# The first quarter of two weight matrices in four equal pieces, its fold by halves, v's sums by pairs of heads, and the opening in a new order

## The chip, the cores and the metric

The kernel runs on one core of a Trainium2 chip. A core has five engines with a queue each: TensorE (PE) for matrix products, VectorE (DVE), ScalarE (ACT) and GpSimd (POOL) for elementwise work and reductions, and SyncE (SP), which here issues the loads and stores. The metric is the device time of one execution in microseconds. The kernel before took 639.45 us, the median of three runs (638.46 to 640.53).

## What is computed

An attention with 32 memory slots per head, over 8 batches, 8 heads, 576 positions and 64 channels, and then a two-layer network on all 4608 tokens. The weights of the network are float64 in memory; q, k, v and phi are float32.

```python
a = exp(phi - max(phi, axis=2)); a = a / (sum(a, axis=2) + 1e-09)
k_m = einsum('bhsm,bhsd->bhmd', a, k)
v_m = einsum('bhsm,bhsd->bhmd', a, v)
scores = matmul(q, k_m.T) / sqrt(64)
attn = exp(scores - max(scores)); attn = attn / (sum(attn) + 1e-09)
x = matmul(attn, v_m)            # as [4608, 512]
h = x @ w_in                     # 512 x 2048
out = maximum(0.01 * h, h) @ w_out
```

## The kernel before, in words

The attention's last product and the first layer are folded into one: per batch b and quarter j of the 2048 inner columns, `fold_products` multiplies v_m (in `vT`) by that quarter of w_in. The up products (`up_products`, L1160 in the opening) then multiply these folded weights by the attention weights `a`, `leaky` (L1169) applies the nonlinearity, and the down products (`down_products`, L1244) multiply by a quarter of w_out and add up in PSUM. Batch 0's first tokens are worked in full float32 in the opening, with the weights as they come in; later groups use pairs of float16 halves.

The weights need work before use. A quarter of w_in or w_out (`weights("i", j)`, `weights("o", j)`) is 128 rows of 2048 float64. It is loaded in pieces of 768, 768 and 512 elements to each of the 128 partitions (`ld`), the low word is converted (`h`, on ScalarE at L392 where `OPENING_ACT` lists the piece, on VectorE at L394 where not), the high word is converted on ScalarE (`y`, L403), and VectorE puts both together into the float32 tile (`t`, the put, L412). `b` sums squares of a finished quarter on ScalarE. The pieces are staged in eight slots of `arena` that are used in turn (`ld_slot`), by q and by the next batch's phi, k and v as well: a load can be issued only when the work that read the slot's last content is done.

Nothing is scheduled by a tool. Every step has a name, and two strings, `OPENING` and `LATER`, list the steps in the order in which they are issued; each engine does its own instructions in that order. `a0.` and `a1.` are steps of the attention of batches 0 and 1: phi, k, v and q loads, `A` the maximum of phi, `B` its exponential, `C` the sums over positions (`C10` for k, `C11` for v, both by `slots_of`, L706), `D` transposes and the copy `vT` (`D5`), `E` the scores (`E10` and `E1`, L879) and their transposes into `t` (`E2`, L890), `S` the softmax in chunks, which ends for the first chunk in the transpose into `a` (`S06`, L969). `f00.1` is the fold of quarter 0 (L1036) and `f00.2` its two copies on ScalarE into `w_mem` (L1453). `u0.P0` is an up product, `u0.V0` its nonlinearity, `u0.O0` its down product. `z.1` and `z.4` are dummy products on PE (L1467), 128 or 512 columns wide, whose result nobody reads. `LATER` lists the rest of the program.

Of the kernel before, what the change touches and what calls it, by code (L numbers as in the profile page):

```python
# [44 lines left out]
o0.t0 f00.2 u0.P1 i1.ld0 i1.h0 o1.ld2 u0.P0 i1.h1 i1.y0 u0.V1 a0.D2 o0.ld1 o0.ld2 i1.y1 u1.P0 i1.h2
o2.ld2 u1.P1 i1.t0 u0.V0 o1.ld1 i1.t2 i1.t1 u0.O0 f01.1 i2.ld2 o0.h1 o1.h2 o0.y1 i2.ld1 u1.V0 o0.y2
o2.h2 o1.y2 o0.t1 a0.S11 o0.h2 i2.y2 f01.2 u1.O0 a0.S12 a0.S13 u0.O1 i2.y1 u1.V1 o1.t2 o0.t2 o1.ld0
i2.ld0 i2.h1 o1.y1 i2.h2 o2.y2 a0.S14 i2.t2 o2.ld0 o2.t2 a0.S15 u2.P0 u2.P1 a0.S16 i2.h0 i3.ld1
o1.h0 i2.t1 a1.phi o1.h1 o1.t1 u2.V0 u1.O1 i2.y0 o1.y0 i2.t0 o2.h0 A0.h i1.b a1.kv1 a1.kv0 o1.t0
u3.P0 u2.V1 i3.y1 u2.O0 o2.y0 i2.b u3.V0 a1.kv2 i3.h1 a0.D4 a1.A1 a1.kv3 a1.A2 a1.A3 u3.P1 a1.B0  # L50
i3.t1 a1.B10 a1.q1 a1.B20 f02.1 o2.t0 u3.O0 f02.2 a1.B3 a1.C10 a1.C2 a1.C30 u5.P0 o0.b a1.C31
o2.ld1 a1.q0 u3.V1 u4.P1 o1.b u5.V0 a1.C4 a1.D11 u4.P0 a1.C3k o2.h1 i3.ld0 a1.D2 A0.l a1.Q1 a1.Q0
a1.D10 a0.S17 o2.y1 i3.ld2 o3.ld0 a1.D3 u4.V0 i3.y0 a1.D5 u2.O1 i3.y2 i3.h0 a1.D4 o2.t1 i3.h2 u4.V1
i3.t0 a2.phi i3.t2 a1.E1 u3.O1 i3.b a1.E21 o3.h0 u4.O0 a1.E20 o3.ld1 ci.1 o2.b a1.S11 a2.A1 ci.2
W03.p o3.y1 a1.S01 o3.h1 o3.t1 o3.ld2 a0.S18 u5.P1 o3.y2 a2.kv2 o3.h2 ci.3 u5.O0 ci.4 o3.t2 u4.O1
o3.y0 e0. o3.t0 W03.h1 u5.V1 W03.l1 a2.A2 a1.S02 W03.h0 e1. a1.S03 W03.l0 o3.s0 o3.b u6.P0 co.1
# [1502 lines left out]
```

## Time and profile before

| What | us |
|---|---|
| median of 3 runs | 639.45 (638.46 to 640.53) |
| the profiled execution, whole | 639.44 |
| its span in the profile | 637.3 |
| PE busy | 628.7 |
| VectorE busy | 526.8 |
| ScalarE busy | 399.2 |
| first up products start | 27.91 |

All other times are read from the profile of one execution, counted from the start of its span. PE is busy for 99% of the span; its busy time includes the dummy products of the opening. The granted clock of PE reads 1.00 of full speed in every stretch.

### The profile page before, as it was taken

The numbers are of one execution on the slowest core, as the hardware profiler recorded it, in microseconds if no ns is written. First come the engines' busy times: TensorE is split into PE (matmuls) and PEld (weight loads), VectorE is DVE, ScalarE is ACT, GpSimd is POOL, SyncE is SP. The second block draws the span as 40 slices with busy tenths as digits, with TensorE's granted clock in tenths as the row PEclk, the third lists the DMA queues.
The fourth block names the chain that finished last, engine by engine and source line by source line (L and its number), as shares of the span: only waits on it lengthen the run. The fifth ranks groups of instructions, "written<-read, shape, count | busy, mean of one in ns | idle before, by whom it ended". The sixth has DMA issues, their size and how long they took to land.

```text
span 637.3 us, 17457 instructions
## 1 busy us (share of the span) xinstructions
PE 628.7 (99%) x7408; PEld 489.2 (77%) x7408; DVE 526.8 (83%) x887; ACT 399.2 (63%) x690; POOL 32.4 (5%) x38
## 2 busy tenths in 40 slices
PE   8999999999999999999999999999999999999997
PEld 4545446665568888888888888889888888998886
DVE  5868899999998999996988887889877886766473
ACT  3799889777757546565566636646655646455471
POOL 0011110110010001000010001100200010000000
PEclk9999999999999999999999999999999999999999
DMA  8999612262343433503332224012242100010101
GB/s 311 405 372 319 245 46 51 75 114 89 103 102 71 150 60 72 170 12 73 71 108 64 55 46 103 19 51 76 84 77 34 36 1 19 17 35 1 35 23 45
DMA packets 85182, 61.18 MB, mean 96 GB/s; under 512 B 62064, under 2 KB 67440, under 8 KB 85104
## 3 DMA queue, kind: packets, MB, share of 16 engines
q1 hardware_dynamic: 84720, 59.80, 33.0%
q8 instruction: 58, 0.95, 0.6%
q10 hardware_dynamic: 384, 0.26, 0.2%
q14 instruction: 20, 0.16, 0.1%
HBM read 50.59 MB, written 9.45 MB: 94 GB/s over the span
## 4 chain that ended last, share of the span: by engine, by line
PE 90%; DMA 3%; DVE 3%; ACT 2%; issue 1%; SPq 1%; DVEq 0%; ACTq 0%
PE po L1354 34%; PE ph L1293 23%; PE po L1244 12%; PE ph L1160 6%; PE ph L1354 6%; PE pa L1036 4%; PE pa L706 3%; DMA arena<-in_moe_w_in_dram 2%; PE pa L863 1%; DMA arena<-in_phi_dram 1%; ACT arena L403 1%; PE ph L879 1%; DVE arena L1323 0%; ACT arena L392 0%; DVE r1k L600 0%
## 5 line engine op out<-in xcount | busy, mean ns | idle before, releaser
L1354 PEld LDWEIGHTS <-arena 128*128 128x128 f16 x2352 | 227.1, 98 | 30.4 <-issue 4.2
L1306 ACT ACTIVATE wi<-ph,g_sc 128x256 f32<-128x256 f32 x224 | 97.6, 472 | 151.8 <-PE ph L1293 148.4
L1293 PE MATMUL ph<-a,w_mem 128*128 128x256 f16 (+3 forms) x1512 | 147.3, 245 | 0.0
L1354 PE MATMUL po<-wo,arena 128*128 128x256 f16 x1008 | 130.3, 273 | 0.1
L1354 PE MATMUL po<-arena 128*128 128x256 f16 x1008 | 130.1, 273 | 0.0
L1293 PEld LDWEIGHTS <-w_mem 128*128 128x128 f16 x1512 | 119.0, 98 | 13.6 <-issue 4.2
L1244 PE MATMUL po<-wo,arena 128*128 128x512 f16 (+1 forms) x348 | 96.4, 425 | 0.0
L1331 DVE TENSOR_TENSOR arena<-arena 128x1024 f16<-128x1024 f32 x56 | 69.5, 1241 | 30.4 <-ACT arena L1327 30.4
L1327 ACT CAST arena<-arena 128x1024 f16<-128x1024 f32 x56 | 58.6, 1046 | 11.6 <-DVE arena L1323 11.1
L1331 DVE TENSOR_TENSOR arena<-wi,arena 128x768 f16<-128x768 f32 x56 | 54.2, 970 | 14.0 <-ACT arena L1327 13.2
L1244 PEld LDWEIGHTS <-arena 128*128 128x128 f16 x276 | 26.2, 98 | 30.4 <-issue 2.5
L1323 DVE TENSOR_TENSOR arena<-wi,arena 128x256 f32<-128x256 f32 x112 | 47.4, 423 | 1.9
L1327 ACT CAST arena<-wi 128x768 f16<-128x768 f32 x56 | 46.5, 833 | 3.8 <-PE po L1354 2.8
L1323 DVE TENSOR_TENSOR arena<-wi 128x256 f32<-128x256 f32 x112 | 45.7, 449 | 3.4 <-ACT wi L1306 2.1
L1354 PE MATMUL ph<-wo,arena 128*128 128x256 f16 x336 | 45.4, 273 | 0.0
L1160 PE MATMUL ph<-a,w_mem 128*128 128x192 f16 (+2 forms) x288 | 42.0, 293 | 0.8 <-ACT w_mem L1453 0.8
L1001 POOL TENSOR_TENSOR a<-t,a 128x1024 f16<-128x1024 f32 (+2 forms) x16 | 22.2, 1404 | 397.7 <-ACT a L996 344.0
L1075 DVE SCALAR_TENSOR_TENSOR w_mem<-pa,w_mem 128x512 f16<-128x512 f32 x40 | 26.3, 680 | 4.0 <-ACT w_mem L1069 4.0
L1160 PEld LDWEIGHTS <-w_mem 128*128 128x128 f16 x264 | 23.4, 98 | 7.3 <-issue 1.6
L1036 PE MATMUL pa<-wi,vT 64*32 64x512 f16 (+1 forms) x704 | 28.9, 420 | 0.0
L1169 ACT ACTIVATE arena<-ph,g_sc 128x384 f32<-128x384 f32 (+1 forms) x32 | 16.7, 525 | 15.6 <-PE ph L1160 12.5
L1069 ACT ACTIVATE w_mem<-pa 128x512 f16<-128x512 f32 x40 | 23.3, 596 | 5.0 <-PE pa L1036 4.1
(229 smaller groups left out, 752.0 us busy)
## 6 DMA issues: line engine op xcount, KB each, us to landing
out_dram<-obs SPq DMA_DIRECT2D x136, 64.0 KB, 1.7
arena<-in_k_dram SPq DMA_DIRECT2D x28, 288.0 KB, 3.7
arena<-in_v_dram SPq DMA_DIRECT2D x28, 288.0 KB, 3.9
arena<-in_q_dram SPq DMA_DIRECT2D x96, 72.0 KB, 2.9
arena<-in_moe_w_in_dram SPq DMA_DIRECT2D x12, 512.0 KB, 8.1
arena<-in_moe_w_out_dram SPq DMA_DIRECT2D x8, 768.0 KB, 8.0
arena<-in_phi_dram SPq DMA_DIRECT2D x7, 576.0 KB, 4.6
arena<-in_q_dram SPq DMA_DIRECT2D x4, 576.0 KB, 6.8
```

What stands on the lines that cost most here:

```text
L1001: nc.gpsimd.tensor_tensor(piece(lo, tb), piece(t2, tb), piece(hi, tb), ALU.subtract)
L1036: nc.tensor.matmul(pf[g][cols, :], lhs, rhs, start=(n == 0), stop=(n == len(passes) - 1), tile_position=(g * D, hh * M),)
L1069: nc.scalar.activation(tiles(halves(w16(b, j), g)[:, 0]), w(g), AF.Copy, scale=ws)
L1075: nc.vector.scalar_tensor_tensor(tiles(t[:, 1]), w(g), ws, tiles(t[:, 0]), ALU.mult, ALU.subtract)
L1160: nc.tensor.matmul(ph[:, t0:t0 + n * sb], lhs, rhs, start=(m == 0), stop=(m == len(seq) - 1))
L1244: nc.tensor.matmul(pos["32" if full(G, u) else G][t], lhs, rhs, start=(f == 2 * u0 and m == 0), stop=(f == 2 * u1 - 1 and m == len(seq) - 1),)
L1293: nc.tensor.matmul(ph[:, t0:t0 + n], lhs, rhs, start=(m == 0), stop=(m == len(seq) - 1))
L1306: nc.scalar.activation(dst, ph, AF.Prelu, scale=g_sc2[:, j:j + 1], alpha=SLOPE)
L1323: nc.vector.tensor_tensor(gt[:, x], y, z, op)
L1327: nc.scalar.copy(dst[:, 0], src)
L1331: nc.vector.tensor_tensor(dst[:, 1], src, dst[:, 0], ALU.subtract)
L1354: nc.tensor.matmul(acc, g[:, x, s, u], rhs, start=(h == 0 and k % NQ == 0 and u == 0 and m == 0), stop=(k % NQ == NQ - 1 and u == 1 and m ...
```

## The change

Quarter 0 of each weight matrix is loaded in four pieces of 512 elements per partition. For w_in a piece is two of the four row blocks by half of the quarter's columns, so the first two pieces hold the first half of the columns; for w_out a piece is one block of 128 rows, and the rows of that quarter are dealt to the partitions in another way (`w_out_0`, `by_tile`). The fourth piece of each has a place of its own outside the eight slots. The fold of quarter 0 is made in two halves of columns with two half copies each (`f00.10`, `f00.11`), and v's sums for two heads at a time (`C110`, `C111`), with v's loads in two steps (`v0`, `v1`). `OPENING` is listed anew, `OPENING_ACT` moves conversions of low words between ScalarE and VectorE; `LATER` is the same. (`half` and the steps `u0.P00` and the like are defined and not listed.)

```diff
-a0.phi0 z.4 a0.phi1 z.4 a0.A10 z.4 a0.A11 a0.k a0.A2 a0.A3 z.1 z.1 a0.B0 a0.B10 a0.B20 a0.B11
+a0.phi0 a0.A10 z.4 a0.phi1 a0.A11 z.4 a0.k z.4 a0.A2 a0.A3 a0.q1 a0.B0 z.4 a0.B10 z.1 i0.ld0 a0.B20
...
 OPENING_ACT = {
-    "i0": (0, 1, 2), "i1": (2,), "i2": (2,), "i3": (2,), "o0": (0, 1, 2), "o1": (0, 1, 2),
-    "o2": (0, 1, 2), "o3": (0, 1, 2),
+    "i0": (0, 1, 2),
+    "i1": (0,),
+    "i2": (),
+    "i3": (2,),
+    "o0": (0,),
+    "o1": (1,),
+    "o2": (0, 2),
+    "o3": (0, 1),
 }
...
+    w_out_0 = w_out.rearrange("(j f p) e -> j p f e", p=P, j=NQ)[0]
+    HQ = FQ // 2
...
         def load(i):
+            if j == 0:
+                n = E
+                st = ld_slot() if i < 3 else at(G_OLD + 4 * 3072 if kind == "i" else W_OLD, 8 * n)
+                st = st.bitcast(I64)
+                if kind == "o":
+                    nc.sync.dma_start(st[:, 0:n], w_out_0[:, i])
+                else:
+                    cs, fs = slice(i % 2 * 2, i % 2 * 2 + 2), slice(i // 2 * HQ, (i // 2 + 1) * HQ)
+                    nc.sync.dma_start(
+                        st[:, 0:n].rearrange("p (c f) -> p c f", c=2), src[:, cs, fs]
+                    )
+                return views(i, st, n)
...
+                steps[f"{name}v{i}"] = lambda i=i: [load_kv(hh, (1,)) for hh in (2 * i, 2 * i + 1)]
...
+            steps[f"{name}C10"] = lambda: slots_of((0,))
             for i in range(2):
-                steps[f"{name}C1{i}"] = lambda i=i: slots_of((i,))
+                steps[f"{name}C11{i}"] = lambda i=i: slots_of((1,), range(2 * i, 2 * i + 2))
...
-    def fold_products(b, j):
+    def fold_products(b, j, f0=0, f1=FQ):
...
-        pf = [ps_a.tile([P, FQ], F32, name="pa") for g in range(NG)]
+        pf = [ps_a.tile([P, f1 - f0], F32, name="pa") for g in range(NG)]
...
-                    fs = slice(hh * FQ, (hh + 1) * FQ)
+                    fs = slice(hh * FQ + f0, hh * FQ + f1)
...
+    def half_products(h):
+        first["f", 0, h] = fold_products(0, 0, h * HQ, (h + 1) * HQ)
+
+    for h in range(2):
+        steps[f"f00.1{h}"] = lambda h=h: half_products(h)
+        for g in range(NG):
+            steps[f"f00.2{h}{g}"] = lambda h=h, g=g: nc.scalar.copy(
+                w32[0][g][:, h * HQ:(h + 1) * HQ], first["f", 0, h][g]
+            )
```

What the new order makes of it is seen at three places. Line numbers of the changed kernel are higher by about 40. The first is PE's queue at the start of the up products (L1160 before, L1203 after); L790 and L830 are x_v's transpose, L1467 and L1526 dummies, L1036 and L1076 the fold, L1244 and L1287 down products. Before:

```order
L790 MATMUL pa<-ident,x_v 128x128
L1467 MATMUL po<-ones 128x512
L1036 MATMUL pa<-wi_89,vT 32x512 x8
L1160 MATMUL ph<-a,w_mem 128x384 x4
L350 MATMUL pa<-mdiag,ones 128x128
L1160 MATMUL ph<-a,w_mem 128x384 x4
L1244 MATMUL po<-wo_91,arena 128x512 x3
L1036 MATMUL pa<-wi_88,vT 32x512 x8
```

And after:

```order
L830 MATMUL pa<-ident,x_v 128x128
L1526 MATMUL po<-ones 128x512
L1076 MATMUL pa<-wi_89,vT 32x256 x8
L1526 MATMUL po<-ones 128x128 x2
L1203 MATMUL ph<-a,w_mem 128x384 x4
L1076 MATMUL pa<-wi_89,vT 32x256 x8
L1287 MATMUL po<-wo_91,arena 128x512 x3
L1203 MATMUL ph<-a,w_mem 128x384 x4
```

Half of the fold now stands behind the first two up products.

The second place is SP's queue from the second half of q on; `wo_92` to `wi_86` are the places of k and v for the four pairs of heads. Before:

```order
L589 DMA arena<-in_q_dram 128x2x576
L382 DMA arena<-in_moe_w_in_dram 128x512
L382 DMA arena<-in_moe_w_in_dram 128x256
L382 DMA arena<-in_moe_w_in_dram 128x512
L555 DMA wo_92<-in_v_dram 128x576
L555 DMA wo_93<-in_v_dram 128x576
L555 DMA wo_94<-in_v_dram 128x576
L555 DMA wi_86<-in_v_dram 128x576
L378 DMA arena<-in_moe_w_out_dram 128x768
```

And after:

```order
L628 DMA arena<-in_q_dram 128x2x576
L402 DMA arena<-in_moe_w_in_dram 128x2x256
L593 DMA wo_92<-in_v_dram 128x576
L593 DMA wo_93<-in_v_dram 128x576
L593 DMA wo_94<-in_v_dram 128x576
L593 DMA wi_86<-in_v_dram 128x576
L402 DMA arena<-in_moe_w_in_dram 128x2x256
L399 DMA arena<-in_moe_w_out_dram 128x512
L402 DMA arena<-in_moe_w_in_dram 128x2x256
L399 DMA arena<-in_moe_w_out_dram 128x512
```

One piece stands ahead of q's second half in both (not shown); v now comes ahead of the other two pieces of the quarter.

The third place is VectorE's queue from the scores' transposes on (L890 before, L930 after); L412 and L449 are puts, L961 and L1001 the scaling, L969 and L1009 the transpose into `a`. Before:

```order
L890 STREAM_TRANSPOSE t_299<-pa 128x96 x3
L944 TENSOR_REDUCE tm<-t_299 128x24
L947 TENSOR_TENSOR t_299<-t_299,tm 128x768
L412 SCALAR_TENSOR_TENSOR wi_89<-arena 128x768
L956 TENSOR_REDUCE ts__399<-t_299 128x24
L957 TENSOR_SCALAR ts__399<-ts__399 128x24
L958 RECIPROCAL ts__399<-ts__399 128x24
L761 TENSOR_SCALAR x_v<-po,r_228 128x64 x2
L961 TENSOR_TENSOR t_299<-t_299,ts__399 128x768
L769 TENSOR_REDUCE l_409<-x_v 128x2
L343 TENSOR_REDUCE m_412<-l_409 128x1
L345 TENSOR_SCALAR mdiag<-ident,m_412 128x128
```

And after:

```order
L984 TENSOR_REDUCE tm<-t_332 128x24
L987 TENSOR_TENSOR t_332<-t_332,tm 128x768
L930 STREAM_TRANSPOSE t_332<-ph 128x96
L930 STREAM_TRANSPOSE t_332<-pa 128x96 x3
L801 TENSOR_SCALAR x_v<-po,r_229 128x64 x2
L996 TENSOR_REDUCE ts__395<-t_332 128x24
L997 TENSOR_SCALAR ts__395<-ts__395 128x24
L998 RECIPROCAL ts__395<-ts__395 128x24
L1001 TENSOR_TENSOR t_332<-t_332,ts__395 128x768
L1009 STREAM_TRANSPOSE a<-t_332 128x768
L429 TENSOR_SCALAR arena<-arena 128x512
L449 SCALAR_TENSOR_TENSOR wo_91<-arena 128x512
```

The last transposes and x_v moved to behind the subtraction, the put and the absolute sums to behind the transpose into `a`.

## Rows read from the trace of the kernel before

**Rows 1.** The page's totals: engine, busy us, share of the span, instructions.

```profile
PE 628.7 (99%) x7408; PEld 489.2 (77%) x7408; DVE 526.8 (83%) x887; ACT 399.2 (63%) x690; POOL 32.4 (5%) x38
```

**Rows 2.** Waits of PE, 27.5 us to the end: total us, times, longest.

```profile
...
PE ph L1160 <- ACT w_mem L1453: 0.8, 1, 0.8
PE pa L641 <- DVE r1k L600: 0.3, 1, 0.3
```

**Rows 3.** PE in order of time: start, us, what, count, [idle before <- releaser].

```profile
0.99 5.49 PE L1467 MATMUL po<-ones 128*128 128x512 f32 x6 [0.99 <-POOL ones L274]
...
12.25 1.88 PE L1467 MATMUL po<-ones 128*128 128x512 f32 x4
...
16.52 0.49 PE L1467 MATMUL po<-ones 128*128 128x128 f32 x2
16.94 0.42 PE L879 MATMUL ph<-wo,kT 32*32 32x288 f32 x1
...
22.51 0.27 PE L706 MATMUL po<-wo,wi 64*32 64x64 f32 x6
...
26.05 1.09 PE L1036 MATMUL pa<-wi,vT 64*32 64x512 f32 x16
27.91 2.85 PE L1160 MATMUL ph<-a,w_mem 128*128 128x384 f32 x8 [0.77 <-ACT w_mem L1453]
...
51.84 0.30 PE L641 MATMUL pa<-ident,r1k 128*128 128x128 f32 x1 [0.32 <-DVE r1k L600]
```

**Rows 4.** VectorE in order of time.

```profile
18.48 0.38 DVE L890 STREAM_TRANSPOSE t<-ph 128x192 f32<-128x192 f32 x1 [0.85 <-PE pa L879]
...
19.58 0.24 DVE L890 STREAM_TRANSPOSE t<-ph 128x96 f32<-128x96 f32 x1
...
20.24 0.91 DVE L944 TENSOR_REDUCE tm<-t 128x24 f32<-128x768 f32 x1
21.18 0.96 DVE L947 TENSOR_TENSOR t<-t,tm 128x768 f32<-128x768 f32 x1
...
23.05 0.95 DVE L956 TENSOR_REDUCE ts__399<-t 128x24 f32<-128x768 f32 x1
...
24.48 0.38 DVE L761 TENSOR_SCALAR x_v<-po,r 128x64 f32<-128x64 f32 x2
24.77 0.95 DVE L961 TENSOR_TENSOR t<-t,ts__399 128x768 f32<-128x768 f32 x1
...
26.34 0.97 DVE L969 STREAM_TRANSPOSE a<-t 128x768 f32<-128x768 f32 x1
...
43.06 0.68 DVE L412 SCALAR_TENSOR_TENSOR wo<-arena 128x512 uint32<-128x512 uint32 x1
...
49.47 2.23 DVE L600 TENSOR_REDUCE r1k<-arena 128x128 f32<-128x1152 f32 x1 [0.42 <-DMA arena<-in_phi_dram]
```

**Rows 5.** ScalarE in order of time, 25 to 28 us.

```profile
25.90 0.69 ACT L403 ACTIVATE arena<-arena 128x512 f32<-128x512 f32 x1
...
27.30 1.05 ACT L1453 COPY w_mem<-pa 128x512 f32<-128x512 f32 x2
```

**Rows 6.** SP's queue in order of time, the load of a1's phi.

```profile
43.77 0.38 SPq L544 DMA_DIRECT2D arena<-in_phi_dram  x1
```

**Rows 7.** Waits of SP's queue, 27 to 50 us.

```profile
SPq L544 <- DVE wo L412: 4.4, 1, 4.4
SPq L382 <- DVE wi L412: 3.8, 2, 3.3
```

**Rows 8.** Stretches: us, busy by engine, granted clock, DMA share, GB/s.

```profile
12.00:32.00 20.00, 18.34 (x274) 10.24 (x275) 17.04 (x35) 15.06 (x24) 0.00 (x0) 1.00 1.03 408
32.00:42.00 10.00, 10.00 (x39) 4.17 (x38) 5.23 (x10) 8.82 (x16) 1.41 (x2) 1.00 0.99 362
42.00:50.00 8.00, 8.00 (x23) 4.10 (x22) 7.10 (x12) 8.00 (x12) 2.06 (x3) 1.00 1.00 365
```

**Rows 9.** The same view, from the transpose into `a` to phi's request; VectorE is third.

```profile
27.30:43.80 16.50, 15.89 (x57) 7.81 (x58) 10.11 (x18) 15.16 (x27) 1.71 (x3) 1.00 1.00 380
```

More of the change, by code (lines that the diff above doesn't have):

```diff
@@ L45 @@
[L45 to L56, printed above, removed]
@@ L410, in put @@
             hi, lo, _ = words.pop(i)
-            c0, n = PIECES[i]
+            t = part(i).bitcast(U32)
+            if len(t.shape) == 3:
+                hi, lo = (x.rearrange("p (c f) -> p c f", c=2) for x in (hi, lo))
             nc.vector.scalar_tensor_tensor(
-                dst.bitcast(U32)[:, c0:c0 + n], hi, 3, lo, ALU.logical_shift_left, ALU.bitwise_or
+                t, hi, 3, lo, ALU.logical_shift_left, ALU.bitwise_or
             )
@@ L460, in weights @@
                     steps[f"{name}{key}{x}"] = lambda fn=fn, x=x: fn(x)
-        for i in range(len(PIECES)):
-            for key, fn in (
-                ("ld", load), ("h", low), ("y", high), ("t", put), ("k", hi_part),
-                ("l", lo_part),
-            ):
-                steps[f"{name}{key}{i}"] = lambda fn=fn, i=i: fn(i)
+        for keys, n in (
+            ((("ld", load), ("h", low), ("y", high), ("t", put)), n_ld),
+            ((("k", hi_part), ("l", lo_part)), len(PIECES)),
+        ):
+            for i in range(n):
+                for key, fn in keys:
+                    steps[f"{name}{key}{i}"] = lambda fn=fn, i=i: fn(i)
         steps[name + "b"] = squares
@@ L691, in _, with slots_of @@
             nc.vector.tensor_tensor(s0, s0, ph[:, :, 8], ALU.add)
-        def slots_of(kinds):
+        def slots_of(kinds, heads=range(HP)):
             if "pk" not in var:
@@ L702, in slots_of @@
             for j in range(KJ):
-                for hh in range(HP):
+                for hh in heads:
                     for g in range(NG):
@@ L1065, in w @@
         def w(g):
-            return tiles(w32[j][g]) if b == 0 and j < Q32 else by_tile(src["w"][g])
+            return tiles(w32[j][g]) if b == 0 and j < Q32 else by_tile(src["w"][g], j)
         def hi_part(g):
@@ L1134, in width, with up_products @@
         return GT if G < G2 - 1 else 2 * P
-    def up_products(G, u, i):
-        ph = ps_h.tile([P, width(G)], F32, name="ph")
+    def up_products(G, u, i, ph=None, block=None):
+        if ph is None:
+            ph = ps_h.tile([P, width(G)], F32, name="ph")
         (b0, tb0), (b1, tb1) = blocks(G)
         sb = width(G) // 2
-        if b0 == b1:
+        if block is not None:
+            parts = [((b0, b1)[block], (tb0, tb1)[block], 1, block * SB)]
+        elif b0 == b1:
             parts = [(b0, tb0, 2, 0)]
@@ L1431, in act, with half @@
             leaky(dst[:, i], first["ph", u, i], 0, u)
+        def half(i, block):
+            gs[0, u] = g_old(u).rearrange("p (i x) -> p i x", i=2)
+            first["ph", u, i] = up_products(0, u, i, first.get(("ph", u, i)), block)
         for i in range(2):
             steps[f"u{u}.P{i}"] = lambda i=i: products(i)
+            if u < 2:
+                for x in range(2):
+                    steps[f"u{u}.P{i}{x}"] = lambda i=i, x=x: half(i, x)
             steps[f"u{u}.V{i}"] = lambda i=i: act(i)
@@ L1447 @@
         steps[f"Y0.{t}"] = lambda t=t: set_aside(t)
-    for j in range(Q32):
+    def half_products(h):
[6 more added lines that the diff above has]
+            )
+    for j in range(1, Q32):
         def products(j=j):
@@ L1452 @@
         steps[f"f0{j}.2"] = lambda j=j: [
-            nc.scalar.copy(tiles(w32[j][g]), by_tile(first["f", j][g])) for g in range(NG)
+            nc.scalar.copy(tiles(w32[j][g]), by_tile(first["f", j][g], j)) for g in range(NG)
         ]
```

46 lines of the change are left out of this document (35 added, 11 removed).

## The prediction

> **What bounds the kernel now.** I read the totals first, then who TensorE (PE) waits for, then the opening in order of time, and last the loads. The totals [rows 1] show PE busy 628.7 of 637.3 us, so there is little to win outside its gaps. The waits [rows 2] say where the gaps are: once the real work has begun, PE waits 0.8 us for the copy of the first folded weights and 0.3 us for a maximum on VectorE. After the opening the program is one row of matmuls without a hole. Hence the time is the moment at which the real products start, plus their work, plus any new hole.
>
> That moment is 27.91 us [rows 3]: the first up products (L1160). Before it PE does dummy products (L1467), scores and sums. Two chains meet there. One is the scores on VectorE, which end with the transpose into `a` at 26.34 + 0.97 = 27.31 [rows 4]. The other is v: its sums are taken on PE from 22.51, then x_v on VectorE (24.48), its transpose and a copy on ScalarE, the fold at 26.05 and the two copies from 27.30, of which the up products need the first [rows 3 to 5].
>
> The third thing to see is what lies behind. The next attention block (a1) needs its phi. It is asked for at 43.77 [rows 6], after a wait of 4.4 us until a staging slot is free [rows 7]. VectorE, idle until it lands, begins the maximum at 49.47, 5.7 us later, and needs 2.23 us [rows 4], and PE stands 0.32 us at 51.84 because of it [rows 3]. So before the change PE and the loads arrive at 51.8 almost together. The DMA share is 1.03, 0.99 and 1.00 from 12 to 50 us [rows 8]: the loads ahead of that phi fill the DMA engines all the time.
>
> **The change, part by part.** Times are of the profiled execution: 639.44 us, of which 637.3 are span and 2.1 lie around it; the median shown is 639.45, so no correction is needed.
>
> The score chain. The dummy between the two score products goes (16.52): the second starts about 0.4 us earlier than 16.94 (16.94 - 16.52) [rows 3]. The transposes then start near 18.05 instead of 18.48. Of them only the first part (18.48 to 19.58, 1.10) stays ahead of the maximum; the other part moves beneath the exponential. From start to start in [rows 4]: 18.05 + 1.10 + 0.94 (20.24 to 21.18) + 1.87 (21.18 to 23.05, subtraction and exponential) = 21.96. The moved transposes (0.66, 19.58 to 20.24) and x_v (0.29, 24.48 to 24.77) follow the subtraction (0.96, from 20.09) and end near 22.0, beneath the exponential, as the put that stood there did. Then come the sum (1.43, 23.05 to 24.48), the scaling (0.95) and the transpose (0.97); the absolute sums between these two (26.34 - 24.77 - 0.95 = 0.62) move behind. The chain ends at 25.3, 2.0 us earlier.
>
> The v chain. Two pieces of 512 KB stand ahead of v, no longer the whole quarter; the other two and a first piece of w_out come behind. That is 1.05 MB less, 2.6 us at 408 GB/s [rows 8], so v, whose sums began at 22.51 [rows 3], can be there near 19.9 at the latest; PE has done the scores at 18.0 and two short dummies by 18.5, and takes the sums in two halves of 0.8. Two long dummies and a short one follow (0.94 each, half of 1.88, and some 0.25 [rows 3]); x_v ends at 22.0. ScalarE has three conversions of 512 elements between the exponential, which ends just ahead of 21.96, and vT; at 0.6 to 0.7 each [rows 5] vT ends near 24.0. The first half of the fold costs half of 1.09 [rows 3], so 24.6, and its two copies some 0.8 (half of 1.05 [rows 5], and the fixed part of each, an estimate): 25.4. The fourth piece stands 0.5 MB, 1.3 us, behind the place that v had; if it is late, vT is late by as much, 0.5 us at most.
>
> So the up products can start near 25.4, 2.5 us earlier. The second half of the fold (0.55) now stands behind that point and was ahead before. All other work of PE up to a1's transpose of the maximum is the same, in another order. PE's lead there is 2.5 - 0.55 = 1.95 us; without the old hole of 0.32 it could do that transpose 2.3 us earlier, at 49.55.
>
> But that transpose can't come before phi has landed plus 2.23 plus 0.14 us [rows 3, 4]. In front of phi stand the same bytes as before: the change moves none of those loads behind it. What can phi gain? At least nothing, if the stream runs as before: 51.84 again. At most what the rate of 12 to 32 us, kept up to the end, would give: 32 to 49.47 moved 10 x 0.362 + 7.47 x 0.365 = 6.35 MB; at 408 GB/s that is 15.6 us, and phi lands 1.9 us earlier [rows 8]. In that stretch SP stood for slots (4.4 and 3.8 us [rows 7]), so fewer requests were under way. The change gives two pieces places of their own outside the eight slots, and the first puts come earlier; but conversions that were ScalarE's now stand on VectorE ahead of the put that frees phi's slot. I take a third of the span between the ends, 0.6 us: the row for the same loads in the same stretch is the nearer one. The first quarter now moves in runs of 2 KB and 4 KB instead of 4 and 6; no row prices that by itself, and I cost it at nothing, with 0.3 us to each side.
>
> VectorE and ScalarE. Nine conversions more, net, go to VectorE (15 instead of 6; ScalarE has seven fewer). One of 512 elements costs less than a put of that size, 0.68 [rows 4]; 0.4 to 0.56 is my estimate, so some 4.5 us, seven of them ahead of phi's slot. VectorE was busy 10.1 of 16.5 us from 27.3 to 43.8 [rows 9]; these 6.4 us of idle time hide them. If that cover is gone, each us of it delays phi's request. Later parts of the opening are listed anew, with the same work; no row tells me of a gain or a loss there, and with PE's gaps at zero a loss is the likelier.
>
> Sum: 639.4 - 0.6 = **638.8 us**. Of the 2.3 us that PE could win, some 1.7 become a hole ahead of a1's transpose.
>
> **The rivals.**
> *The lead goes through.* If the loads of 32 to 50 us run as those of 12 to 32, phi lands 1.9 us earlier, PE stands only 0.4 us, and the time is 637.5; with slots freed earlier still, all of the 2.3 comes through: 637.1. For it: SP's waits for slots [rows 7]. Against it: the share is 0.99 and 1.00 while the rate is low [rows 8], so the engines had requests, and their packets took longer.
>
> *VectorE holds phi's slot (slower).* SP asks for phi only after the put that empties its slot, before from 43.06 to 43.74 [rows 4]. In the new order VectorE does, from the end of the scores to that put, ten puts of 512 (0.68), two of 768 (0.96, the length of the subtraction of 768), ten conversions (0.4 to 0.56) and some 2.2 us of attention: 15.5 us of work against 10.1. With no wait it ends at 40.8; with all 6.4 us of idle time as before [rows 9] at 47.2, 3.4 us late. Phi then takes between 1.4 us (its 0.59 MB at 408 GB/s, an empty stream) and its 5.7: it lands at 48.6 to 52.9. At two thirds of the way, 51.5, it is 2.0 us later than before, and at the upper end 3.4: 641.4 to 642.8, say 641.8. It decides from the point where phi lands after 49.5. Against it: the idle time was waiting for data and for ScalarE, which the added work overlaps.
>
> *The clock falls in the hole (slower).* The first three dummies took 5.49 / 3 = 1.83 us each, later ones 1.88 / 2 = 0.94 [rows 3]: PE begins at the pace of the lower of its two levels, 1.2 GHz, and works at the higher one, 2.4, from the scores on. A hole of 1.7 us is longer than any behind the start in the trace (0.8 [rows 2]). If the level fell there and rose again as at the start, 5.5 us at half pace would cost 2.7 us: 641.5. The Trainium skill, page "TensorE: Matmul & The Clock Gate", section "HAM oscillation — how this bites in real kernels", says that waits for DMA between bursts of matmuls can bring the low clock back each time. By that rule the time would be this rival's; the trace agrees only in the slow start, and with holes of up to 0.8 us the granted clock stays 1.00 [rows 8].
>
> *The start doesn't move.* If v or the fourth piece is late, the first products start near 27: the time is 639.4.
>
> **How the numbers follow.** Forecast 0.63, with a range of its own of 638.0 to 639.7; the lead goes through 0.17; VectorE 0.11; the clock 0.04; the start unmoved 0.05. What a measurement can tell from no change is about 0.3%, 1.9 us: 637.5 and 641.4 are the borders. Faster takes most of the first rival and a little of the forecast's edge: 0.17. Slower takes most of the second rival, which has a cheap end too, and half of the third: 0.11. The same: 0.72. The range of 637.0 to 640.9 takes in the forecast, the first rival and the unmoved start; the two slow ones are mostly left out.
>
> **What would show it.** Right: the scores' last transpose ends near 25.3 and the first up products start near 25.4; a hole of 1 to 2 us on PE ahead of a1's first transpose, released by VectorE, which itself waits for phi's DMA; that transpose at 50.5 to 51.8, and from there the old row of matmuls. Wrong: no such hole (the loads were not the limit), a maximum of a1 that stands behind a put and not behind its DMA, new holes after 55 us, or a granted clock under 1.00 behind the hole.

## The result, and the profile after

The changed kernel takes 643.41 us, the median of six runs (642.31 to 645.66), beside 639.7 us for the kernel before, now in six runs as well: the ratio is 1.0061, with a 95% interval of 1.0041 to 1.0081. It is slower by 3.7 us, where the forecast was 638.8 us with a range up to 640.9. The execution in the profile took 642.31 us, of which 640.2 are span: 2.9 us more span than before [rows 1].

```profile
PE 626.8 (98%) x7412; PEld 487.4 (76%) x7412; DVE 531.7 (83%) x898; ACT 394.2 (62%) x687; POOL 32.1 (5%) x38
```

PE is busy for 1.9 us less, as the opening holds 12.8 us of dummies instead of 16.3, and the span is longer all the same: PE waits for longer. Its waits, from 10 us to the end, against [rows 2]:

```profile
PE po L745 <- issue: 2.6, 1, 2.6
PE pa L745 <- issue: 1.4, 3, 0.6
PE po L1287 <- DVE wo L449: 1.3, 1, 1.3
...
PE pa L680 <- DVE r1k L639: 0.2, 1, 0.2
```

Two of them are new: 2.6 us inside v's sums (L745, L706 before), for which the profile finds no releaser ("issue"), and 1.3 us at a down product, released by a put on VectorE. The wait for phi's maximum, which the forecast saw grow to 1.7 us, has become smaller. PE in order of time, which answers to [rows 3]:

```profile
22.66 0.75 PE L745 MATMUL po<-wo,wi 64*32 64x64 f32 x37 [2.61 <-issue]
...
26.45 0.66 PE L1076 MATMUL pa<-wi,vT 64*32 64x256 f32 x16
...
27.92 2.85 PE L1203 MATMUL ph<-a,w_mem 128*128 128x384 f32 x8 [0.16 <-ACT w_mem L1504]
30.70 0.66 PE L1076 MATMUL pa<-wi,vT 64*32 64x256 f32 x16
...
51.06 2.84 PE L1287 MATMUL po<-wo,arena 128*128 128x512 f32 x6 [1.32 <-DVE wo L449]
54.11 0.30 PE L680 MATMUL pa<-ident,r1k 128*128 128x128 f32 x1 [0.21 <-DVE r1k L639]
```

The first up products start at 27.92, which is where they started before (27.91), and not at 25.4. The sums of v begin at 17.92 and run without a wait for data from 18.49, as forecast (18.5). The trace records each product of the sums as two passes, 144 in all, and with 37 of these still to do PE stops at 20.05 and goes on at 22.66. From the start to a1's first transpose it now takes 26.19 us instead of 23.93: the second half of the fold adds 0.59 (30.70 to 31.29), the hole at 51.06 adds 1.32, the smaller wait for the maximum gives back 0.11, and the 0.46 that are left lie in the starts and ends of groups of products, which change more often now. So a1's transpose is 2.27 us late. Of the 2.9 us these are the greater part; the other 0.6 come later, 0.5 of them in a1's and later batches' own sums (issue: 1.4 us instead of 0.9).

VectorE in order of time, against [rows 4]:

```profile
23.45 0.47 DVE L801 TENSOR_SCALAR x_v<-po,r 128x64 f32<-128x64 f32 x2 [2.36 <-PE po L745]
23.84 0.94 DVE L996 TENSOR_REDUCE ts__395<-t 128x24 f32<-128x768 f32 x1
...
26.36 0.98 DVE L1009 STREAM_TRANSPOSE a<-t 128x768 f32<-128x768 f32 x1
...
44.68 1.32 DVE L449 SCALAR_TENSOR_TENSOR wo<-arena 128x512 uint32<-128x512 uint32 x1
...
48.60 2.41 DVE L449 SCALAR_TENSOR_TENSOR wo<-arena 128x768 uint32<-128x768 uint32 x1
...
51.80 2.17 DVE L639 TENSOR_REDUCE r1k<-arena 128x128 f32<-128x1152 f32 x1
```

x_v stands ahead of the scores' sum in the new order. It needs v's sums, so VectorE stands still for 2.36 us at the hole, and the scores, whose own work was done in time, end at 27.34. The put that frees phi's slot ends at 46.00 and took 1.32 us instead of 0.68; the put of 768 at 48.60 took 2.41 instead of 0.96, and PE waits for it at 51.06. GpSimd works beside both: from 44.50 to 45.45 on a multiplication of the softmax (L1001), then on a subtraction:

```profile
48.30 1.89 POOL L1164 TENSOR_TENSOR w_mem<-a,w_mem 128x768 f16<-128x768 f32 x1 [2.86 <-ACT w_mem L1162]
```

The maximum at 51.80 starts right behind a put. Phi is asked for 2.25 us later than before [rows 6]. It lands 5.2 us after that (the last number of its row), at 51.2, while the maximum of the kernel before could start at 49.47:

```profile
46.02 0.38 SPq L582 DMA_DIRECT2D arena<-in_phi_dram  x1
```

```profile
arena<-in_phi_dram SPq DMA_DIRECT2D x1, 576.0 KB, 5.2
```

The loads, against [rows 8]: SP stands up to 5.7 us for a put on VectorE before it can issue a load (before up to 4.4 [rows 7]), and the stream runs thin from 30 to 32 us (share 0.62), where it was full before.

```profile
12.00:32.00 20.00, 16.29 (x278) 9.14 (x279) 14.59 (x30) 8.83 (x20) 0.00 (x0) 1.00 1.00 378
32.00:42.00 10.00, 10.00 (x41) 4.64 (x41) 8.45 (x18) 9.93 (x17) 0.83 (x1) 1.00 0.95 330
...
30.00:32.00 2.00, 2.00 (x21) 0.81 (x20) 0.69 (x2) 1.20 (x5) 0.00 (x0) 1.00 0.62 180
```

**What the hole could be.** The last of v's loads releases the first sums at 18.45, so all data is there, and nothing in the profile releases PE at 22.66. One more thing has to be there for a matmul: the instruction itself. The page's table of DMA queues has a row for it (packets, MB, share):

```profile
q8 instruction: 58, 0.95, 0.6%
```

58 packets of 16 KB. PE has 2 x 7412 = 14,824 matmuls and weight loads, 256 for each packet, and no other engine has as many instructions: this queue brings PE's program, in blocks of 256. Each short fp32 product of the sums is four of them, two recorded passes and their two weight loads. The packets share the 16 DMA engines with the loads. One of them lies in the hole, in the stretch from 20.2 to 21.4 us:

```profile
q8 instruction: 1, 0.02, 5.7%
```

5.7% of 16 engines for 1.2 us are 1.1 us of one engine. That is theory A in the expectations: PE has used up the instructions it holds, and the next block is late because of the weight loads. Its rivals: the conversions that moved between ScalarE and VectorE make everything late (B), GpSimd beside VectorE's puts is what costs the time (C), or the hole belongs to the products of those 37 passes, by their operands or their place in PSUM (D). F and G are about phi's slot, below.

### The profile page after: what moved, and what is told of

It is laid out like the page before. It is cut to its first block, busy times and chain, and to the rows that moved or that the text cites. A ratio compares the mean times of both kernels' runs of the same rounds, so it can differ in the third digit from the quotient of the medians.

```text
span 640.2 us, 17468 instructions
## 1 busy us (share of the span) xinstructions
PE 626.8 (98%) x7412; PEld 487.4 (76%) x7412; DVE 531.7 (83%) x898; ACT 394.2 (62%) x687; POOL 32.1 (5%) x38
## 4 chain that ended last, share of the span: by engine, by line
PE 90%; DVE 3%; DMA 2%; ACT 2%; issue 1%; SPq 0%; DVEq 0%; ACTq 0%
PE po L1397 34%; PE ph L1336 23%; PE po L1287 12%; PE ph L1203 6%; PE ph L1397 6%; PE pa L1076 4%; PE pa L745 3%; DMA wi<-in_v_dram 2%; PE pa L903 1%; DVE wo L449 1%; DMA wi<-in_k_dram 1%; ACT wi L454 1%; ACT arena L438 0%; PE po L1526 0%; DVE arena L1366 0%
## 5 line engine op out<-in xcount | busy, mean ns | idle before, releaser
L1287 PE MATMUL po<-wo,arena 128*128 128x512 f16 (+1 forms) x348 | 96.8, 426 | 1.3 <-DVE wo L449 1.3
L1287 PEld LDWEIGHTS <-arena 128*128 128x128 f16 x276 | 26.2, 98 | 30.4 <-issue 3.3
L1203 PE MATMUL ph<-a,w_mem 128*128 128x192 f16 (+2 forms) x288 | 42.0, 294 | 0.2 <-ACT w_mem L1504 0.2
L1076 PE MATMUL pa<-wi,vT 64*32 64x512 f16 (+2 forms) x720 | 29.1, 415 | 0.0
L1203 PEld LDWEIGHTS <-w_mem 128*128 128x128 f16 x264 | 23.3, 98 | 7.7 <-issue 1.9
L1212 ACT ACTIVATE arena<-ph,g_sc 128x384 f32<-128x384 f32 (+1 forms) x32 | 16.7, 524 | 15.9 <-PE ph L1203 12.7
```

The source lines that it names most:

```text
L1076: nc.tensor.matmul(pf[g][cols, :], lhs, rhs, start=(n == 0), stop=(n == len(passes) - 1), tile_position=(g * D, hh * M),)
L1203: nc.tensor.matmul(ph[:, t0:t0 + n * sb], lhs, rhs, start=(m == 0), stop=(m == len(seq) - 1))
L1287: nc.tensor.matmul(pos["32" if full(G, u) else G][t], lhs, rhs, start=(f == 2 * u0 and m == 0), stop=(f == 2 * u1 - 1 and m == len(seq) - 1),)
```

## The experiments

Where a run was timed, its ratio is to the kernel before on the same chip. The letters a0.C110 and a0.C111 are the two halves of v's sums.

### The loads pause while the block is due

The three pieces that follow v are asked for only after the scores' maximum, behind a tiny memset on VectorE.

```diff
-... a0.v1 i0.ld2 o0.ld0 a0.C111 i0.t1 i0.ld3 a0.E20 a0.S01 a0.S02 a0.E21 a0.C110 i0.y2 a0.S03
+... a0.v1 a0.C111 i0.t1 a0.E20 a0.S01 a0.S02 a0.E21 gate i0.ld2 o0.ld0 i0.ld3 a0.C110 a0.S03 i0.y2
+    steps["gate"] = lambda: nc.vector.memset(at(slots_used[0] % 8 * IO, IO)[:, 0:2], 0.0)
```

> The changed kernel, but the two pieces of w_in and the one of w_out that follow v are asked for only when the maximum of the scores is done (about 21 us), so the DMA queues run empty between about 18.5 and 21 us. PE's instructions are those of the changed kernel. Theory A (the instruction block waits in the queues behind the loads): the block that landed at about 22.4 us lands at 18 to 19.5, the hole of 2.6 us inside v's sums is gone or under 0.5, and the sums end by 20.8. The pieces come about 3 us later, and so does the rest: no gain in time is expected from this kernel (642 to 646). Theory D, or a fixed time for every block whatever the loads do: the hole stays at 2.2 to 2.9 us and ends near 22.7.

The queues are empty from 18 us (the last two columns: share and GB/s), and the block comes in the stretch from 17.6 to 18.9:

```profile
18.00:20.00 2.00, 1.59 (x108) 1.47 (x108) 1.93 (x4) 0.00 (x0) 0.00 (x0) 1.00 0.00 0
```

```profile
q8 instruction: 1, 0.02, 5.2%
```

PE's hole stands ahead of the same 37 passes, and is 0.42 us:

```profile
20.01 0.75 PE L745 MATMUL po<-wo,wi 64*32 64x64 f32 x37 [0.42 <-issue]
```

PE's instructions and data are those of the changed kernel; only the loads beside them are gone, and the hole ends 2.65 us earlier. So the loads set when the block comes, as A has it, and D, which had 2.2 to 2.9 us, misses. The place of the hole is the same here; two runs below show what moves it. The time itself was missed: 649.36 us in its one run, since the pieces came so late that PE stood for 6.4 us ahead of the first fold, and the granted clock fell to 0.50 in that hole.

### A third of the sums left out

Of batch 0's sums over v three of the nine position slices are left out, 48 recorded passes of 144; the rest is the changed kernel.

```diff
+            kn = KJ - 3 if b == 0 and kinds == (1,) else KJ
-            for j in range(KJ):
+            for j in range(kn):
```

> The changed kernel, with 3 of the 9 slices of positions left out of batch 0's v sums (the result for batch 0 is then wrong): 48 of their 144 recorded products go. Theory A (PE ran out of instructions in the middle of the v sums, because a block of 256 instructions comes some 6 us after the one before it is begun while the loads fill the DMA engines): with 192 instructions fewer to issue there, of which 73 stood behind the hole, the 2.6 us hole before 22.66 is gone, x_v is made near 21.5, the first up products start at 25.2 to 26.0 instead of 27.92, a1's first transpose comes 1.5 to 2.3 us earlier than 54.11, and the time falls by 1.5 to 2.5 us, to the time before the change or just above. Theory B (the conversions moved to VectorE hold a1 back, whatever the start): the start moves, but a1's first transpose stays at 53.5 to 54.1 and the time within 0.5 us of the changed kernel's.

The 48 passes are 96 instructions with their weight loads, not the 192 that the expectation names. 641.91 us (639.2 to 647.74, 12 runs); 1.0049 (1.0026 to 1.0072). PE in order of time:

```profile
25.29 2.82 PE L1204 MATMUL ph<-a,w_mem 128*128 128x384 f32 x8 [0.54 <-DVE a L1010]
...
48.83 2.84 PE L1288 MATMUL po<-wo,arena 128*128 128x512 f32 x6 [1.74 <-DVE wo L449]
51.88 0.30 PE L680 MATMUL pa<-ident,r1k 128*128 128x128 f32 x1 [0.21 <-DVE r1k L639]
...
57.56 1.80 PE L746 MATMUL pa<-arena 64*32 64x128 f32 x110
61.88 0.47 PE L746 MATMUL pa<-arena 64*32 64x128 f32 x8 [2.52 <-issue]
```

The sums have no hole, and the start comes at 25.29: the forecast's 25.4 was right for a kernel without the hole. The hole has moved: 2.52 us at 59.4, in the next batch's sums, where another block now ends. Counted in order of time, 705 instructions of PE (matmuls, weight loads and a few waits) are recorded ahead of the hole in the changed kernel and 1217 ahead of this one: 512 more, two blocks of 256. So it goes by the count of instructions. B falls too: a1's transpose comes 2.23 us earlier, at 51.88. The time fell by less than expected. The new hole stands in it, and behind that hole the granted clock reads 0.50 from 61.8 to 65.2 us.

Yet 51.88 is no gain over the kernel before (51.84), and the loads aren't the reason here. VectorE:

```profile
46.37 2.40 DVE L449 SCALAR_TENSOR_TENSOR wo<-arena 128x768 uint32<-128x768 uint32 x1
...
49.56 2.17 DVE L639 TENSOR_REDUCE r1k<-arena 128x128 f32<-128x1152 f32 x1
```

The loads from 32 to 42 us (the last two columns: share and GB/s), and phi's request with the time to its landing:

```profile
32.00:42.00 10.00, 10.00 (x42) 4.80 (x41) 8.43 (x17) 9.67 (x16) 0.83 (x1) 1.00 1.03 406
```

```profile
43.81 0.38 SPq L582 DMA_DIRECT2D arena<-in_phi_dram  x1
```

```profile
arena<-in_phi_dram SPq DMA_DIRECT2D x1, 576.0 KB, 4.3
```

In this run the loads move 406 GB/s from 32 to 42 us (before 362 [rows 8], in the changed kernel 330), and phi lands at 48.1, 1.4 us earlier than before the change. The maximum starts only at 49.56, behind VectorE's puts, and one of these takes 2.40 us beside GpSimd. No run has both the fewer sums and GpSimd out of the way.

### More instructions ahead of the sums

The two short dummies ahead of v's sums become sixteen of 32 columns.

```diff
-... a0.E10 i0.t0 a0.E1 z.1 z.1 i0.y1 a0.v1 ...
+... a0.E10 i0.t0 a0.E1 z.0 i0.y1 a0.v1 ...
```

> The changed kernel, but the two short dummies ahead of v's sums (128 columns each) become sixteen of 32 columns: 56 hardware instructions more, the same data and the same waits. Theory A (PE has used up the instructions it holds, and the next block of them lands at a fixed time): the hole inside v's sums comes some 28 recorded products earlier, so that about 65 of the 144 stand behind it and not 37, and PE goes on at nearly the same time as before, 22.4 to 22.9 us. Theory D (the hole belongs to those products, by their operands or by the place in PSUM): the hole stays ahead of the last 37 products, and all of it moves by what the dummies take more.

642.16 us in one run. It told less than it should: the dummies took 4.68 us, so that PE reached the sums at 21.59 and the place of the hole only when the block was there. There is no hole in the sums, which speaks against D, but where it would have moved wasn't seen. The clock fell to 0.50 (the third number from the end) in the midst of them. PE in order of time, and the stretch:

```profile
16.98 4.68 PE L1532 MATMUL po<-ones 128*128 128x32 f32 x32
```

```profile
19.60:26.40 6.80, 6.80 (x157) 6.05 (x157) 2.30 (x8) 2.96 (x5) 0.00 (x0) 0.50 1.04 402
```

### x_v behind the scaling

The dummies that stand after v's sums go ahead of them, which gives the block time, and x_v goes behind the scaling on VectorE.

```diff
-... a0.E1 z.1 z.1 i0.y1 ... a0.S03 z.4 o0.h0 z.1 i0.h2 z.4 i0.y3 a0.C31 a0.D11 a0.D5 a0.S04 a0.S05 z.4 f00.10
+... a0.E1 z.1 z.1 z.4 z.1 z.4 i0.y1 ... a0.S03 o0.h0 i0.h2 i0.y3 a0.S04 a0.S05 a0.C31 a0.D11 a0.D5 f00.10
```

> The changed kernel with another order at one place: the three dummies behind the v sums stand ahead of them, the dummy ahead of the fold goes, and VectorE makes x_v behind the scaling instead of ahead of the sum, so that it doesn't stand for PE's hole. Theory A: the hole stays (it hangs on the number of PE's instructions, not on what stands there), the v sums end near 23.4 as before, but the scores' last transpose ends near 25.0 instead of 27.34, the first up products start near 26.0, and the time falls by 1.5 to 2.0 us. Theory B: start earlier, a1's first transpose and the time as in the changed kernel (within 0.5 us).

641.49 us (640.9 to 645.17, 9 runs); 1.0047 (1.003 to 1.0063). The hole is 1.3 us and stands ahead of other passes, 43 instead of 37, while the instructions recorded ahead of it are 705 as in the changed kernel: six passes of dummies now come first. That is what D can't give. The scores end at 25.02 instead of 27.34, and the first up products start at 26.38. But they take 4.11 us instead of 2.85, at a granted clock of 0.50, and the win of the start is gone by the next row (30.42, 30.70 in the changed kernel):

```profile
22.61 0.86 PE L745 MATMUL po<-wo,wi 64*32 64x64 f32 x43 [1.29 <-issue]
...
26.38 4.11 PE L1203 MATMUL ph<-a,w_mem 128*128 128x384 f32 x8
30.42 0.66 PE L1076 MATMUL pa<-wi,vT 64*32 64x256 f32 x16
```

```profile
25.60:29.00 3.40, 3.40 (x8) 2.21 (x9) 2.12 (x4) 1.21 (x3) 0.00 (x0) 0.50 1.03 405
```

a1's transpose stands at 53.81, 0.30 earlier than in the changed kernel, and the gain of 1.5 to 2.0 us that A expected isn't there.

### The old split of the conversions

The new order with the old table of what ScalarE converts.

```diff
 OPENING_ACT = {
-    "i0": (0, 1, 2), "i1": (0,), "i2": (), "i3": (2,), "o0": (0,), "o1": (1,), "o2": (0, 2), "o3": (0, 1),
+    "i0": (0, 1, 2), "i1": (2,), "i2": (2,), "i3": (2,), "o0": (0, 1, 2), "o1": (0, 1, 2), ...
```

> The changed kernel with the old split of the low words' conversions (18 on ScalarE, the fourth pieces and the rest on VectorE) and the new order. Theory B: VectorE has some 4 us less to do ahead of a1's maximum, the put that frees phi's slot ends near 44 instead of 46.0, a1's first transpose comes 1 to 2 us earlier and so does the end. Theory A: the hole and the start (27.9) stay, ScalarE gets 5 us more and is in the way of its own conversions: no gain, or up to 2 us slower.

648.44 us (646.81 to 649.07, 4 runs); 1.0144 (1.0124 to 1.0164). The hole is 3.17 us, the start is at 31.52, and there are new waits for puts; the clock is 0.50 from 22.5 to 29.3. So the old split wins nothing in the new order, against B. It doesn't price the conversions by themselves, as the start and the clock moved with it.

```profile
PE po L1281 <- DVE wo L443: 4.0, 2, 2.9
PE po L739 <- issue: 3.2, 1, 3.2
```

### GpSimd's part later

GpSimd's share of batch 0's low halves (L1164) is moved behind u3's last nonlinearity; the rest is the changed kernel.

```diff
-... a1.kv0 A0.h o2.h0 ... a1.C30 u3.V1 o2.ld1 ...
+... a1.kv0 o2.h0 ... a1.C30 u3.V1 A0.h o2.ld1 ...
```

> The changed kernel with the float16 halves of a's first part made some 13 us later, so that GpSimd's subtraction (48.30 to 50.19) no longer runs beside VectorE's put of 48.60, which took 2.41 us instead of 0.9. Theory C (that collision is a cost of its own): the put takes 0.95, PE's 1.32 us hole ahead of the down product at 51.06 shrinks to 0.3 at most, a1's maximum starts with phi's landing near 51.2 instead of 51.80, and the time falls by 0.5 to 1.0 us. Theory A alone: the start stays at 27.9 and the time falls by no more than 0.3.

643.46 us (642.47 to 645.55, 6 runs); 1.0076 (1.0056 to 1.0096). The put takes 0.94 us and the hole at the down product is gone, so the collision is real, as C has it; but the maximum then waits for phi's DMA, PE waits 1.13 us for the maximum, and the time is the same:

```profile
48.33 0.94 DVE L449 SCALAR_TENSOR_TENSOR wo<-arena 128x768 uint32<-128x768 uint32 x1
...
50.99 2.16 DVE L639 TENSOR_REDUCE r1k<-arena 128x128 f32<-128x1152 f32 x1 [0.85 <-DMA arena<-in_phi_dram]
```

```profile
53.30 0.30 PE L680 MATMUL pa<-ident,r1k 128*128 128x128 f32 x1 [1.13 <-DVE r1k L639]
```

### The sums around the dummies, with GpSimd's part later or as changed

All three groups of long dummies stand between the two halves of the sums, and x_v stands behind the scaling.

```diff
-... a0.E21 a0.C110 i0.y2 a0.S03 z.4 o0.h0 z.1 i0.h2 z.4 i0.y3 a0.C31 a0.D11 a0.D5 a0.S04 a0.S05 z.4 f00.10 z.1
+... a0.E21 z.4 z.4 z.4 a0.C110 i0.y2 a0.S03 o0.h0 i0.h2 i0.y3 a0.S04 a0.S05 z.1 z.1 a0.C31 a0.D11 a0.D5 z.1 f00.10 z.1 z.1
```

> The changed kernel with its opening mended by what the traces showed: all three groups of long dummies stand between the two halves of v's sums, so that PE, which has few instructions to get through there, is busy until the next block lands; x_v stands behind the scaling on VectorE; and GpSimd's share of batch 0's low halves comes after the last nonlinearity of u3, away from VectorE's put of 768. Theory A: no hole over 0.5 us inside v's sums or ahead of them, first up products at 25.6 to 26.6, the granted clock 1.00 throughout the opening, a1's first transpose at 51.5 to 52.5, and a time of 638.5 to 640.5, so about 3 us under the changed kernel and level with the kernel before. If the waits for ScalarE and VectorE, which come from the new places of the conversions, were the cause instead: the hole at u2's down products and later ones stay, and the time stays at 642 to 644.

> The run with the sums around the dummies, but GpSimd's share of batch 0's low halves stands where the changed kernel has it. If the collision of GpSimd with VectorE's put of 768 (2.41 us instead of 0.95) costs time: a hole of 0.8 to 1.8 us ahead of u2's down products, and 0.5 to 1.5 us more than the run without it. If it is hidden because PE waits at a1's transpose anyway for phi: the same time within 0.5 us.

With GpSimd's part later: 641.11 us (639.13 to 642.77, 12 runs), 1.0028 (1.0014 to 1.0041). As changed: 641.11 us (640.41 to 643.86, 9 runs), 1.0037 (1.0024 to 1.0051). The hole in the sums is gone (0.2 us in the second), the clock is 1.00, and the start is at 26.41 and 26.66. The ratio falls by 0.3%, 2 us, yet not to 1: a1's transpose stands at 52.87 and 52.78, a microsecond later than before the change, though the start is 1.3 to 1.5 us earlier. Both runs miss the 638.5 to 640.5 us that A expected. The first run:

```profile
26.41 2.85 PE L1203 MATMUL ph<-a,w_mem 128*128 128x384 f32 x8 [0.16 <-ACT w_mem L1504]
...
48.95 2.84 PE L1287 MATMUL po<-wo,arena 128*128 128x512 f32 x6 [0.43 <-DVE wo L449]
52.87 0.30 PE L680 MATMUL pa<-ident,r1k 128*128 128x128 f32 x1 [1.07 <-DVE r1k L639]
```

And the second, where the long put makes its hole, and the wait for the maximum is shorter by as much:

```profile
49.74 2.84 PE L1287 MATMUL po<-wo,arena 128*128 128x512 f32 x6 [1.26 <-DVE wo L449]
52.78 0.30 PE L680 MATMUL pa<-ident,r1k 128*128 128x128 f32 x1 [0.19 <-DVE r1k L639]
```

So GpSimd's collision costs no time between these two. In the first the maximum waits for phi, asked for at 45.39; in the second phi is asked for at 44.72 and lands at 49.9, and the maximum starts at 50.48 behind the puts. From the first up products to phi's request 18.1 to 19.0 us pass in the changed kernel, in the run with fewer sums (25.29 to 43.81) and in these two; before it were 15.9 (43.77 - 27.91).

### Phi's slot freed earlier, without the hole and with it

The put that frees phi's slot (o2.t2) and its conversion (o2.y2) come some 4 us earlier.

```diff
-... u1.V1 a0.S11 i2.y2 ... i2.ld0 o2.y2 o2.ld0 i2.h2 ... u2.P1 o2.t2 o1.h1 ...
+... u1.V1 o2.y2 a0.S11 i2.y2 ... i2.ld0 o2.t2 o2.ld0 i2.h2 ... u2.P1 o1.h1 ...
```

> The run with the sums around the dummies, and one more edit: the put of the third piece of w_out's third quarter, which frees the slot of the next batch's phi, stands right behind the put that frees the slot ahead of it, and its conversion on ScalarE right behind u1's second nonlinearity; both stood some 4 us later, behind a softmax chunk. Theory F (the second half of the loss is VectorE's queue: from the first up products to phi's request took 15.9 us before the change and 18.1 to 19.0 in every run of the new order): phi is asked for at 41 to 42 us and not at 45.39, the maximum no longer waits for phi's DMA and starts at 49.0 to 49.8, the hole of 1.07 us at a1's first transpose is gone or under 0.3, that transpose comes at 51.3 to 51.9, and the time falls by 1 to 1.5 us to 639.2 to 640.5. Theory G (the load stream is full, so that an earlier request lands no earlier, as the forecast had it): phi lands at 50.0 or later all the same, the transpose stays at 52.5 or later and the time at 641.

> The same early put, and GpSimd's part later, but the changed kernel's own order ahead of the up products, with its hole of 2 to 2.6 us in v's sums: beside the run with GpSimd's part later alone (643.46) and the two runs without the hole it makes a square of hole or none, put late or early. Theory F: phi is asked for at 42.5 to 43.5, the hole of 1.13 us at a1's first transpose is gone or under 0.3, the transpose comes at 52.0 to 53.0 and the time at 641.5 to 643, some 2 us above the run without the hole, because PE then has no wait left in which the late start could hide. Theory G: transpose at 53 or later, 643 to 644.

Without the hole: 640.66 us (638.83 to 642.13, 10 runs), 1.0019 (1.0009 to 1.0029). With it: 645.64 us (642.31 to 646.98, 6 runs), 1.0089 (1.0068 to 1.011). SP and then VectorE, without the hole:

```profile
41.09 0.38 SPq L582 DMA_DIRECT2D arena<-in_phi_dram  x1
```

```profile
49.80 2.17 DVE L639 TENSOR_REDUCE r1k<-arena 128x128 f32<-128x1152 f32 x1 [0.45 <-DMA arena<-in_phi_dram]
```

PE of the run with the hole:

```profile
27.73 2.85 PE L1203 MATMUL ph<-a,w_mem 128*128 128x384 f32 x8 [0.17 <-ACT w_mem L1504]
...
53.62 0.30 PE L680 MATMUL pa<-ident,r1k 128*128 128x128 f32 x1 [1.18 <-DVE r1k L639]
```

Phi is asked for 4.30 us earlier (45.39 to 41.09), and the maximum, which still waits for its DMA, starts 0.77 us earlier (50.57 to 49.80): phi takes 8.7 us now. With the hole it is asked for at 42.45, 3.6 us earlier than in the changed kernel, and the maximum starts at 51.31, no earlier than in the run with GpSimd's part later alone (50.99). F falls: in these two pairs a request put 3.3 to 4.3 us earlier lands 0.8 us earlier or 0.3 us later. G comes nearer, though without the hole its landing at 50.0 or later and its transpose at 52.5 or later are missed too (49.80 and 52.12). With or without the early put the times differ by less than their intervals; without the hole they are lower by 0.5% and 0.7%. The last kernel, all mended, is still 1.3 us slower than the kernel before, so nothing here beats it.

## Why the prediction was wrong, step by step

**The step that failed** is "PE ... takes the sums in two halves of 0.8", beneath the score chain. The data was there (18.45, the forecast said 19.9 at the latest), the first half took its 0.8, and in the second PE stood 2.6 us for its own instructions. No term of the sum had them in it. Seven kernels have such a hole. In each of them PE goes on at the same distance from the end of an instruction packet (from the trace's records of packets):

| run | packet ends | PE goes on | between |
|---|---|---|---|
| changed kernel | 21.34 | 22.66 | 1.32 |
| loads pause | 18.78 | 20.01 | 1.23 |
| third of the sums left out | 60.32 | 61.88 | 1.56 |
| x_v behind the scaling | 21.33 | 22.61 | 1.28 |
| old split | 22.18 | 23.46 | 1.28 |
| GpSimd's part later | 21.07 | 22.40 | 1.33 |
| early put, with hole | 21.13 | 22.48 | 1.35 |

In the kernel before, a packet ends at 22.17, and PE passes the same count of 705 instructions at 23.49, 1.32 us later. The sums began at 22.51 there, and dummies, 18 passes in 4.18 us, stood ahead:

```profile
18.39 4.18 PE L1467 MATMUL po<-ones 128*128 128x128 f32 x18
```

So the same limit was there, and hidden. From the border 256 instructions ahead of it (PE passes that at 17.29 before and at 16.47 in the changed kernel) to this one it is 6.2 us in both, and 3.45 us in the run where the loads pause. An earlier v could not bring this block earlier. The Trainium skill, page "Runtime: NRT & Kernel Launch", section "Instruction fetch mechanics", has instructions come in 16 KiB blocks of 256 over a DMA queue of the sequencer's own, and calls the cost of a block's border mostly hidden. The size agrees with the 58 packets; that the cost is hidden doesn't hold here, where short products follow each other while loads fill the DMA engines. Why PE needs 1.2 to 1.6 us more behind a packet's end no run shows.

**The score chain** was sized rightly and ordered wrongly: it ends at 25.15 in the run with fewer sums (forecast 25.3). In the changed kernel it ended at 27.34, because x_v stands ahead of the sum in VectorE's queue and passed the wait for v's sums on. The text took x_v to end at 22.0 and named nobody who would wait if it didn't; that was the place to ask.

**The start** therefore didn't move. The rival that said so had 0.05 and gave 639.4; it looked for a late v or a late fourth piece, and neither was late. **The second half of the fold** behind the start cost 0.59, forecast 0.55.

**The loads that bound a1's phi** were sized with 0.6 us of gain, from the row in which they move 362 GB/s. In the run with fewer sums they move 406 and phi lands 1.4 us earlier, which is nearly the condition of the first rival (1.9 us). Where PE's clock held, phi's landing goes with the start: 48.1 with the start at 25.29, 49.8 to 50.5 with 26.35 to 26.66, and 51.0 to 51.3 with 27.66 to 27.92. So the hole cost the loads too: with the start unmoved, the new order brings phi 1.7 us later than the old one. Which step of the new order does that no run takes apart.

**VectorE's puts** had no term in the sum, as idle time was to hide the added work, and the second rival priced them at 0.68 and 0.96 us. Beside GpSimd they took 1.32 and 2.41. With fewer sums the maximum stood behind them and not behind phi, and the transpose came at 51.88. By its numbers phi's landing would have allowed 50.5 (48.1 + 2.23 + 0.14, an estimate). No run shows whether the forecast's 638.8 would come with these puts out of the way.

**VectorE holds phi's slot** was the rival that came nearest in time (641.4 to 642.8; the profile has 642.31), with its mark, phi landing after 49.5 (51.2), and with the sign that the prediction calls wrong for itself, a maximum right behind a put. VectorE's busy time from 27.3 to 43.8 grew from 10.1 [rows 9] to 12.4 us. But the put that frees phi's own slot isn't the cause: coming some 4 us earlier, it doesn't move the time. What is left are the slots ahead of it in the queue, and no run moved their puts.

**The clock** got 0.04, for a hole of 1.7 us at phi. In the profile of the changed kernel it reads 1.00. Its six runs have a mean granted clock of 0.997 three times (643.18 to 645.66 us) and of 0.999 or 1.000 three times (642.31 to 643.64). Over all kernels with a hole of 1.3 us or more in batch 0's sums, a mean of 0.997 or less stands in 22 of 31 runs; in the three without such a hole anywhere in 1 of 31. The run with fewer sums, whose hole stands at 59.4, has it in 7 of 12. So these holes bring the low clock with them often, which fits that the median lost 3.7 us where the profile lost 2.9: the three runs at 0.999 or 1.000 have a median of 642.59, the other three of 644.05. What decides in which run it falls stays open.

**What stays open**: the 1.3 us by which the last kernel is slower than the one before. Its a1 transpose is 0.28 us late (52.12); the rest comes behind it, in waits of 0.3 us for ScalarE, 0.5 us for VectorE and 1.8 instead of 0.9 us of "issue" in later sums. They weren't taken away one by one, and that execution, at 642.13 us, was the slowest of its ten.

## What to carry to other kernels

A wait that the profile calls "issue", in a burst of short products, is to be looked up in the row of the instruction queue: when a burst is moved to an earlier time, its instructions must be there as well as its data, and long products between two parts of it give them time. A step that is put ahead in a queue hands its wait to all that stand behind it, so each moved step needs the question who waits if its input is late. And where the loads ahead of a request set its landing, an earlier request alone gains little; what moved the landing here was the start of the work that frees the slots of those loads.

## What the runs showed of the hardware

- PE's program comes in packets of 16 KB, one for 256 instructions; a packet takes 1.1 us in a full load stream as in an empty one (5.7% of 1.2 us and 5.2% of 1.3 us of 16 engines), but starts 2.5 us later in the full one (20.2 and 17.7 us), and PE goes on 1.2 to 1.6 us after its end. One block took PE 6.2 us in the full stream (17.29 to 23.49 before, 16.47 to 22.66 after) and 3.45 us where the loads paused (16.56 to 20.01).
- Sixteen fp32 dummies of 32 columns took 4.68 us, 146 ns for each of their 32 recorded passes; the granted clock fell to 0.50 in the midst of them, at 19.6 us, though PE was busy without a break.
- A put of 768 with two inputs took 2.41 us beside GpSimd's subtraction of 1.89 us, and 0.94 alone.
